# One second-level sum of an attention job by accumulating DMAs, a lead of three jobs, DMA transposes before the feed-forward, and six W2 buffers

## The chip, the cores and the metric

The kernel runs on one core of a Trainium2 chip, in one launch. The core has a matrix engine (TensorE, PE in the profile), a vector engine (VectorE, DVE), an activation engine (ScalarE, ACT), GpSimd (POOL) and a queue engine (SyncE, SP) that here only issues DMAs. Each of them runs its own list of instructions in order; semaphores make one wait for another. 16 DMA engines move data. The metric is the device time of one execution in microseconds (us).

## The reference

One transformer layer on 2048 tokens of width 1024, all in bf16, with 32 heads of width 32 and a feed-forward width of 3584:

```python
qkv = (layernorm(x) @ wqkv).reshape(B, S, 3, H, Dh)            # H = 32, Dh = 32
p = softmax(q @ k.T * Dh ** -0.5)                              # per head, 2048 x 2048
h = x + (p @ v) @ wo
h2 = h + gelu_tanh(layernorm(h) @ w1 + b1) @ w2 + b2           # F = 3584
```

The layer norms have no weights. Rounding of the variance and of its root follows bf16.

## The kernel before

**A planner writes the instruction lists.** The kernel first describes its whole work as tasks with an engine, a cost, a latency, the buffers that they read and write, and a priority (`Graph.add`). `Graph.schedule` then plays these tasks through in time and writes down the order on each engine; `assign` turns dependences into semaphore waits. What runs on the chip is that fixed order, with waits: if something is late on the chip, the engine that waits for it stands still, and all that follows in its list with it. Two tables of digits (`PV_BEGIN`, `PV_MUST`) and two of shifts (`GROUP_SHIFT`, `PRIO_SHIFT`) steer the order; they have no other effect.

**Attention.** A job is one block of 256 queries (`qb`, 0 to 7) with one group of four heads (`g`, 0 to 7): 64 jobs. A job has 8 rounds of 256 keys. In a round PE writes the scores of four heads with 8 matmuls (`qk`, line 941), ACT takes the exponential in two instructions of 128 x 1024 (line 952) into a buffer PT, and PE multiplies by V with 8 matmuls (`pv`, line 996). The scores use PSUM banks 0 to 5 as three units of two banks; a round takes two units, so PE can be about half a round ahead of ACT. Banks 6 and 7 serve everything else.

**Row sums.** The softmax denominators come from matmuls with a matrix of ones (`den`, line 1036). To need fewer of them, DVE first adds the two halves of a round's PT into a sum buffer PS (the first-level sum, line 1013), then adds PS buffers in pairs (the second-level sum, line 1019). A job has seven first-level sums, for rounds 0 to 6, and three second-level ones, for rounds 0+1, 2+3 and 4+5. Round 7 goes into `den` directly, with 8 matmuls instead of 4 per sum. There are three PS buffers. `Job.pv` writes this; `DIRECT` says how many of the last rounds go directly.

**Lead.** At the start the tokens come in 16 tiles of 128. DVE computes the layer norm of a tile (lines 715 to 741), PE transposes it (line 763), ACT or DVE copies it to `xnT` (lines 770 and 772; `LEAD_ACT` lists the ten tiles that ACT copies), and PE projects Q, K and V of head group 0. With each pair of tiles two more half-chunks of keys are there, and the rounds of jobs (0,0) and (1,0) are put in as their keys come. 50 warm-up matmuls (line 1262) stand in front. After the lead `ORDER` names the jobs that run between the remaining projections.

**Feed-forward.** It is spread as background work over the attention of later query blocks, one block of 256 tokens (a unit) at a time: `wo` (output projection and residual), `ln2` (second layer norm, PE transposes, and a DVE copy to `hnT`, line 772), `ffn1` (14 weight blocks of 512 KB, DVE adds the bias, and gelu with DVE and one ACT tanh), `ffn2` (two halves of 7 weight blocks of 512 KB, in a ring of seven buffers `a_w2r`). The last unit's feed-forward stands alone at the end, and so does part of the one before; its gelu runs on ACT. GpSimd only computes a power for the layer norms (line 736).

Of the kernel before, what the change touches and what calls it, by code (L numbers as in the profile page):

```python
# [13 lines left out]
BF = dt.bfloat16  # L14
F32 = dt.float32
# [21 lines left out]
class Task:  # L37
    __slots__ = ("eng", "fns", "occ", "lat", "deps", "prio", "kind", "mode", "left", "succ", "ready", "done",
                 "order", "inc", "flow", "value", "grp", "lane", "waits", "bytes", "acq", "rel", "whole")

    def __init__(self, eng, fns, occ, lat, prio, kind, mode):
        self.eng, self.fns, self.occ, self.lat = eng, fns, occ, lat
        self.prio, self.kind, self.mode = prio, kind, mode
        self.deps = set()
        self.succ = []
        self.left = 0
        self.ready = 0.0
        self.done = None
        self.order = None
        self.inc = False  # L50
        self.flow = None
        self.value = 0
        self.lane = None
        self.waits = ()
        self.bytes = 0
        self.grp = None
        self.acq = None
        self.rel = None
        self.whole = None


class Graph:
# [7 lines left out]
    def __init__(self, n_lanes):  # L70
        self.tasks = []
        self.regions = {}
        self.n_lanes = n_lanes
# [36 lines left out]
    def schedule(self, pick_pe, pool, switch=(0.11, 0.106, 0.1), dma_rate=340.0, dma_first=1.6, dma_tail=1.0, dma_issue=0.42,  # L110
# [9 lines left out]
        lanes = [None] * self.n_lanes  # L120
        state = {"mode": None, "dma": 0.0, "pace": 0.0}
# [21 lines left out]
        while n < total:  # L143
# [5 lines left out]
            for e in self.ENGS:  # L149
                while free[e] <= now + 1e-9:  # L150
# [12 lines left out]
                    else:  # L163
                        t = min(rd, key=lambda x: (x.prio, num[x]))
                        if up and t.prio > 0:

                            for (rt, _, u) in up[:6]:
                                if u.prio < t.prio and rt < now + 0.6 * t.occ:
# [17 lines left out]
                    if e == E.SP:  # L186
# [14 lines left out]
                        state["dma"] = s0 + t.bytes / dma_rate / 1e3  # L201
                        t.done = state["dma"] + dma_tail
# [34 lines left out]
    def assign(self, flows, lane_flows):  # L237

        for t in self.tasks:
            best = {}  # L240
            keep = set()
            for d in t.deps:
                if d.eng == E.SP:
# [8 lines left out]
        lane_n = [0] * len(lane_flows)  # L252
        for e in self.ENGS:
            c = 0
            for t in self.seqs[e]:
                if e == E.SP:
# [3 lines left out]
                    t.value = 16 * lane_n[t.lane]  # L260
                else:
# [43 lines left out]
        for i, s in enumerate(lane_flows):  # L305
            self.sems[("L", i)] = s

# [22 lines left out]
    def emit(self, e, obj):  # L330
        for t in self.seqs[e]:
# [5 lines left out]
            if t.inc:  # L337
                ins.then_inc(self.sems[t.flow], 16 if e == E.SP else 1)


PV_BEGIN = "6887668783765478677666734877585674766834855865775635885656674536"
PV_MUST = "2563656375427345237632753323452322425663763553734473555222232667"
GROUP_SHIFT = (
        "0:-229 1:131 2:136 6:-161 8:-202 9:133 11:142 14:17 15:-143 16:-115 17:-197 18:-131 20:-226 22:18 "
        "26:-18 28:-97 32:-17 33:177 34:-29 39:56 40:-11 42:55 44:53 45:81 46:22 48:243 50:-360 51:-22 "
        "55:-161 56:-142 57:-12 61:-20 66:-4 68:-18 69:18 72:-25 73:-7 76:-9 78:-61 83:-51 84:5 88:-36 "
        "89:-80 91:-37 92:-13 93:-18 94:6 95:125 98:-125 100:-193 101:-23 104:132 105:226 106:91 111:401 "
        "112:505 113:205 117:-165 118:182 120:-316 121:-313 122:-8 123:-383 124:-11 127:54 131:-14 133:-43 "
        "134:-32 135:-435 136:-33 138:-391 141:-7 145:-13 150:102 160:-184 163:3 165:232 166:-25 167:-29 "
        "169:-162 174:-10 175:592 176:-1 177:626 178:17 179:99 180:-167 182:-21 183:116 184:-46 185:11 "  # L350
        "186:24 187:-51 197:-74 198:-215 199:13 200:81 201:-20 202:4 207:-50 208:-4 209:172 211:-27 214:118 "
        "215:-55 216:-45 219:385 230:-13 231:14 232:-7 233:72 234:-5 235:78 236:-65 238:135 239:-593 240:29 "
        "241:-111 244:-185 245:112 247:-121 248:22 250:39 251:104 252:15 261:50 264:-4 268:220 270:-530 "
        "271:5 272:-920 273:1 274:-176 276:-54 277:91 279:24 281:31 293:171 294:13 295:123 296:-33 298:-6 "
        "299:111 300:113 301:2 305:321 308:34 310:17 311:10 313:52 315:-85 326:3 328:-4 329:-160 330:-11 "
        "331:-184 333:-150 334:102 335:-44 338:9 339:-99 341:74 342:48 344:-2 345:-172 347:170 349:-26 "
        "350:-28 352:-23 354:63 355:-74 356:-11 ")
PRIO_SHIFT = (
        "0:1 2:1 4:-1 6:-3 67:-1 68:-4 69:1 70:1 72:1 78:1 79:-3 80:1 81:-3 83:1 84:1 104:-2 125:-1 128:-3 "
        "129:-2 130:-1 132:-1 133:-1 154:1 167:-1 176:1 183:-1 187:-1 188:-1 228:-1 230:-1 234:-2 239:-4 "  # L360
        "250:-2 260:-3 264:-2 266:-2 276:-3 282:-1 307:-2 310:1 322:-3 330:-2 332:1 334:1 335:-1 344:1 353:1 "
        "356:-1 360:-1 369:2 370:1 371:2 373:-2 375:-1 378:-1 381:-1 406:2 415:3 417:1 418:2 420:-1 423:-1 "
        "426:3 427:1 446:4 462:1 511:-1 545:2 579:3 613:1 623:1 624:-1 627:1 637:-3 646:-1 649:1 651:1 "
        "652:-1 655:1 657:5 661:1 665:1 667:-1 670:1 672:1 676:1 684:2 686:1 698:-1 702:2 708:-1 710:-1 "
        "720:-1 722:-1 725:1 737:1 739:-1 753:-2 754:3 765:1 766:-2 772:-4 774:-1 778:2 788:1 789:-1 791:-1 "
        "792:-2 801:-1 810:3 870:1 936:-3 969:2 1003:-1 1020:-1 1037:-1 1040:1 1066:1 1086:-1 1089:-2 "
        "1097:-1 1102:-1 1103:-1 1114:-1 1126:1 1127:2 1130:2 1137:1 1138:3 1139:-1 1140:-1 1150:1 1168:-2 "
        "1186:1 1254:-1 1262:-1 1264:-1 1274:-3 1279:-1 1282:-1 1288:-1 1294:-1 1302:1 1303:1 1305:-1 "
        "1314:-1 1322:-2 1326:-2 1340:-1 1344:1 1346:-1 1358:-2 1394:1 1484:1 1485:-1 1494:2 1497:2 1508:-1 "
        "1515:-1 1519:1 1520:-1 1521:-1 1526:1 1528:-1 1531:1 1537:1 1540:2 1549:-2 1555:-3 1561:-3 1571:-1 "  # L370
        "1572:-1 1575:-3 1584:-1 1593:-1 1620:-1 1637:-2 1654:-1 1701:3 1710:-1 1716:-1 1732:1 1737:-1 "
        "1739:-3 1740:1 1742:-1 1748:1 1753:2 1756:-1 1760:-2 1762:-2 1765:2 1766:-1 1774:-1 1777:-2 1778:-1 "
        "1780:-1 1788:-1 1790:2 1791:3 1801:-1 1810:1 1828:-1 1837:-1 1854:1 1871:1 1888:2 1905:1 1908:1 "
        "1918:-1 1919:2 1928:1 1931:-2 1940:1 1943:1 1946:2 1949:3 1954:2 1955:-1 1956:-2 1968:1 1970:1 "
        "1982:1 1992:2 1998:1 2006:-1 2007:1 2008:1 2105:-1 2130:-1 2136:2 2142:1 2159:3 2166:1 2170:1 "
        "2171:1 2172:-1 2173:-1 2174:1 2187:-1 2196:-1 2200:1 2206:1 2211:-1 2212:1 2222:-1 2224:-1 2226:-2 "
        "2262:1 2271:-1 2274:2 2276:-2 2279:-1 2284:1 2288:1 2296:1 2297:-1 2300:3 2315:1 2319:-1 2320:-4 "
        "2323:-1 2326:1 2328:-2 2340:1 2343:-2 2348:1 2349:-3 2355:1 2361:-1 2367:-1 2373:1 2375:-3 2386:1 "
        "2398:1 2408:1 2410:-1 2420:-1 2440:-2 2465:-3 2493:1 2494:-1 2498:-7 2503:1 2512:-1 2513:-1 2516:-2 "
        "2517:-1 2518:1 2521:-1 2522:3 2544:1 2574:-1 2576:-2 2586:1 2595:1 2618:1 2636:-1 2655:-1 2656:3 "  # L380
# [1153 lines left out]
```

## Time and profile before

Three runs took 1078.71, 1082.22 and 5466.11 us; the median is 1082.22 us.

| | |
|---|---|
| profiled execution | 1079.89 us, its span 1078.0 us |
| instructions recorded | 38343 |
| busy: TensorE, ScalarE, VectorE, GpSimd | 1037.0, 1016.2, 887.6, 18.8 us |
| first exponential starts, last one ends | 17.69 us, 1017.66 us |
| VectorE, second-level sums (line 1019) | 191, 130.8 us |
| TensorE clock granted | 1.00 throughout |
| DMA moved | 173.93 MB, mean 161 GB/s |

Busy time is a union of intervals: an ACT instruction's record overlaps the next one's, so 1016.2 us of busy time do not say that no instruction came late. The page also shows the chain that ended last (followed back from the end), groups of instructions by line with the idle time before them and what ended it, and the median time of each kind of DMA from issue to landing.

### The profile page before, as it was taken

How to read it: one execution, taken by the hardware profiler on the slowest of the kernel's cores; microseconds unless marked ns; L12 is line 12 of the kernel's file. 1: busy time of each engine (PE TensorE's matmuls, PEld its weight loads, DVE VectorE, ACT ScalarE, POOL GpSimd, SP SyncE). 2: the span in 40 equal slices, each digit the busy share in tenths (PEclk: the TensorE clock that was granted, in tenths of full speed). 3: DMA queues.
4: the chain of work that ended last, by engine and by line, in shares of the span. 5: the costliest groups of instructions: out<-in, count | busy, mean ns of one | idle time of the engine just before them, and what ended most of it. 6: DMA issues, size and time to landing. Idle time of an engine off the chain costs nothing.

```text
span 1078.0 us, 38343 instructions
## 1 busy us (share of the span) xinstructions
PE 1037.0 (96%) x17162; PEld 586.8 (54%) x17162; DVE 887.6 (82%) x1737; ACT 1016.2 (94%) x1121; POOL 18.8 (2%) x35
## 2 busy tenths in 40 slices
PE   7889999999999999999999999999999999999998
PEld 5546555554446645654466457456645644564483
DVE  8888677777789997998789979988997997997711
ACT  4999999999999999999999999999999999999850
POOL 2000000000000000000000000000000000000000
DMA  7910010005656575754686667558575755987640
GB/s 196 256 60 3 13 49 2 2 2 175 205 153 204 149 224 167 220 164 132 222 259 183 189 197 203 163 173 260 150 222 184 210 150 162 290 258 236 192 153 20
DMA packets 265492, 173.93 MB, mean 161 GB/s; under 512 B 26864, under 2 KB 259952, under 8 KB 264944
## 3 DMA queue, kind: packets, MB, share of 16 engines
q1 hardware_dynamic: 265328, 171.48, 53.1%
q8 instruction: 135, 2.21, 0.8%
q14 instruction: 29, 0.24, 0.1%
HBM read 161.09 MB, written 10.35 MB: 159 GB/s over the span
## 4 chain that ended last, share of the span: by engine, by line
ACT 85%; PE 10%; DVE 3%; DMA 2%; issue 0%; SPq 0%; DVEq 0%
ACT PT L952 79%; PE ps L672 5%; ACT tg L1215 4%; PE ps L669 3%; ACT PX L952 1%; PE ps L941 1%; DMA a_w1r<-in_B_w_dram 1%; DVE st L715 1%; ACT xnT L770 1%; DMA xrb<-in_A_x_dram 0%; PE ps L996 0%; DVE PS L1013 0%; DMA a_w1r<-in_A_wo_dram 0%; DVE xb L741 0%; DVE gT L1192 0%
## 5 line engine op out<-in xcount | busy, mean ns | idle before, releaser
L952 ACT ACTIVATE PT<-ps 128x1024 bf16<-128x1024 f32 x1008 | 937.4, 1148 | 5.4 <-PE ps L941 5.2
L1013 DVE TENSOR_TENSOR PS<-PT 128x1024 bf16<-128x1024 bf16 x439 | 297.4, 684 | 78.1 <-ACT PT L952 52.1
L941 PE MATMUL ps<-QT,KT 32*128 32x256 bf16 x4096 | 203.6, 273 | 13.6 <-ACT PT L952 9.9
L996 PE MATMUL ps<-PT,V 128*32 128x256 bf16 x4032 | 160.5, 273 | 2.9 <-DVE gT L1192 1.1
L941 PEld LDWEIGHTS ps<-QT,KT 32*128 32x128 bf16 x4096 | 60.8, 92 | 170.0 <-ACT PT L952 157.8
L669 PE MATMUL ps<-hnT,a_w1r 128*128 128x256 bf16 x1197 | 148.1, 273 | 1.8 <-DMA a_w1r<-in_B_w_dram 0.7
L1019 DVE TENSOR_TENSOR PS<-PS 128x1024 bf16<-128x1024 bf16 x191 | 130.8, 685 | 3.4
L669 PE MATMUL ps<-a_w2r,gT 128*128 128x512 bf16 x510 | 125.7, 380 | 3.7 <-DVE hnT L772 1.2
L669 PEld LDWEIGHTS ps<-hnT,a_w1r 128*128 128x128 bf16 x1197 | 109.2, 98 | 35.3 <-issue 20.3
L996 PEld LDWEIGHTS ps<-PT,V 128*32 128x32 bf16 x4032 | 100.9, 96 | 37.5 <-issue 6.3
L666 PE MATMUL ps<-a_w2r,gT 128*32 128x512 bf16 x1096 | 80.2, 382 | 0.4 <-DVE gT L1192 0.2
L669 PEld LDWEIGHTS ps<-a_w2r,gT 128*128 128x128 bf16 x510 | 43.8, 98 | 61.9 <-issue 15.0
L1036 PE MATMUL ps<-PS,ones 128*32 128x256 bf16 x1020 | 70.5, 274 | 0.8 <-DVE PS L1013 0.5
L1192 DVE TENSOR_TENSOR gT<-ps,b1f 128x512 bf16<-128x512 f32 x98 | 66.7, 684 | 4.8 <-PE ps L669 2.4
L666 PE MATMUL ps<-hnT,a_w1r 128*32 128x256 bf16 x1484 | 54.5, 274 | 1.7 <-DMA a_w1r<-in_B_w_dram 0.6
L1215 ACT ACTIVATE tg<-tg 128x1024 bf16<-128x1024 bf16 x49 | 55.6, 1148 | 0.0
L669 PE MATMUL ps<-xnT,Wall 128*128 128x512 bf16 (+1 forms) x241 | 51.9, 345 | 2.5 <-ACT xnT L770 1.6
L669 PE MATMUL ps<-Wall,xnT 128*128 128x256 bf16 x345 | 45.6, 274 | 1.4 <-DVE KT L819 0.8
L666 PEld LDWEIGHTS ps<-hnT,a_w1r 128*32 128x32 bf16 x1484 | 36.3, 96 | 13.4 <-issue 11.2
L666 PE MATMUL ps<-xnT,Wall 128*32 128x512 bf16 x540 | 39.1, 381 | 0.6 <-DVE KT L819 0.6
L1244 DVE SCALAR_TENSOR_TENSOR b_ost<-ps,hch 128x512 bf16<-128x512 f32 x4 | 2.8, 692 | 44.7 <-PE ps L672 44.7
L669 PEld LDWEIGHTS ps<-Wall,xnT 128*128 128x128 bf16 x345 | 31.2, 98 | 12.7 <-issue 5.1
(101 smaller groups left out, 998.0 us busy)
## 6 DMA issues: line engine op xcount, KB each, us to landing
a_w2r<-in_B_w_dram SPq DMA_DIRECT2D x105, 512.0 KB, 4.8
a_w1r<-in_B_w_dram SPq DMA_DIRECT2D x98, 512.0 KB, 4.8
a_w1r<-in_A_wo_dram SPq DMA_DIRECT2D x32, 512.0 KB, 4.5
b_w1r<-in_B_w_dram SPq DMA_DIRECT2D x14, 512.0 KB, 5.0
a_w1r<-in_A_wqkv_dram SPq DMA_DIRECT2D x11, 512.0 KB, 4.0
xrb<-in_A_x_dram SPq DMA_DIRECT2D x16, 256.0 KB, 4.1
Wall<-in_A_wqkv_dram SPq DMA_DIRECT2D x16, 256.0 KB, 4.6
hch<-in_A_x_dram SPq DMA_DIRECT2D x16, 256.0 KB, 4.4
```

Of the source, the lines that this page charges most:

```text
L666: fns.append(lambda p, j=j: p.matmul(psum[32 * j:32 * j + 32, bi(bank), c0:c1], lhsT[:, 32 * j:32 * j + 32], rhs, start=start, stop=stop, ...
L669: t.whole = lambda p: p.matmul(psum[:, bi(bank), c0:c1], lhsT, rhs, start=start, stop=stop, skip_group_check=True)
L672: t = pe(lambda p: p.matmul(psum[:, bi(bank), c0:c1], lhsT, rhs, start=start, stop=stop), occ, reads=reads, writes=[bb(bank)], mode="full" ...
L715: return dve(lambda v: v.bn_stats(st_l[:, i, 6 * c:6 * c + 6], src), 0.6, reads=[B_src], writes=[B_stl[i][c]], prio=prio)
L941: return p.matmul(psum[:, 2 * us[h // 2] + h % 2, n * i:n * i + n], KT[32 * h:32 * h + 32, g, k0:k0 + P], QT[32 * h:32 * h + 32, qs, 0:n], ...
L952: act(lambda a, u=u, k=k: a.activation(pt(s)[:, k, :, :], psum[:, 2 * u:2 * u + 2, :], ACT.Exp, bias=0.0, scale=SCALE), 1024, reads=[B_ps[ ...
L996: fns.append(lambda p, i=i, h=h: p.matmul(psum[32 * h:32 * h + 32, bi(bank), 0:nq], V[:, g, nk * r + i, 32 * h:32 * h + 32], pt(s)[:, h // ...
L1013: dve(lambda v: v.tensor_tensor(PS[:, n, :, :], pairs[:, :, 0:256], pairs[:, :, 256:512], ALU.add), c_dve(1024, 2), reads=[B_PT[2 * s], B_ ...
L1019: dve(lambda v: v.tensor_tensor(PS[:, n, :, :], PS[:, n, :, :], PS[:, m, :, :], ALU.add), c_dve(1024, 2), reads=[B_PS[n], B_PS[m]], writes ...
L1036: fns.append(lambda p, h=h, rhs=rhs, i=i: p.matmul(psum[32 * h:32 * h + 32, bi(bank), nq:2 * nq], ones32[:, :], rhs, start=False, stop=las ...
L1192: drop(dve(lambda v: v.tensor_tensor(gT[:, fc:fc + 2, cs], psum[:, bi(bank), 0:2 * n].rearrange("p (f c) -> p f c", f=2), b1f[:, fc:fc + 2 ...
L1215: act(lambda a: a.activation(t, t, ACT.Tanh, bias=0.0, scale=math.sqrt(2.0 / math.pi)), c, reads=B_t, writes=B_t, prio=-1)
```

## The change

1. **Accumulating DMAs.** After the early jobs (`soft_from`, which holds for the last 44 of 64 jobs) the second-level sum of rounds 0+1 is no longer a DVE instruction. GpSimd issues a DMA from one sum buffer to the other that adds (`add_by_dma`), with six semaphores of its own; the planner books it with 1 us on GpSimd and 524,288 bytes on the DMA engines.
2. **Two more sum buffers**, `PSX`, used by the same jobs: five in all.
3. **Six `a_w2r` buffers instead of seven**, to make room. `w2_blocks` still loads seven blocks for a half before its matmuls are recorded, so the seventh goes into the first's buffer, and the matmuls for the first four 128-row chunks of W2 wait for the seventh load and read its data: of each half in that ring rows 0 to 511 of W2 are left out and rows 3072 to 3583 are used in their place as well. The number of instructions, loads and bytes is that of seven blocks. The one half that has another ring (`b_w2r`, the last unit's first) is untouched.
4. **DMA transposes.** For seven of eight units `ln2` no longer transposes with PE and copies with DVE; SP issues a transposing DMA from the normalised tile to `hnT` (14 in all).
5. **A new lead.** Three jobs, (0,0), (1,0) and (2,0), instead of two; their 24 rounds go into `den` directly, with no DVE sums. ACT copies four tiles to `xnT` instead of ten, and two K, two Q and one V half-blocks instead of one K and one Q. The first tile is loaded in two parts and the second straight after it, ahead of the Q weights; the first Q half-block and all K half-blocks are projected in pieces of 128 columns; 34 warm-up matmuls. Fourteen exponential buffers (PX) beside the PT ring instead of eight.
6. **Order.** `ORDER` has jobs of query blocks 2 and 3 for head group 1 as well, and takes the last three groups of blocks 0 and 1 one block after the other; all four tables of the planner are new.

```diff
@@ attention sums
     def DIRECT(qb, g):
-        return 0 if qb < DA else 1
+        return 16 if g == 0 and qb < DLEAD else 1
...
-                n = cnt["ps"] % NS
+                n = cnt["ps"] % (NS + NSX if soft_from else NS)
...
-                    dve(lambda v: v.tensor_tensor(PS[:, n, :, :], PS[:, n, :, :], PS[:, m, :, :], ALU.add), c_dve(1024, 2),
-                        reads=[B_PS[n], B_PS[m]], writes=[B_PS[n]], prio=-2)
+                    if soft_from and r < 2:
+                        add_by_dma(ps(n), ps(m), P * 4096, [B_PS[n], B_PS[m]], [B_PS[n]], -2)
+                    else:
+                        dve(lambda v: v.tensor_tensor(ps(n), ps(n), ps(m), ALU.add), c_dve(1024, 2),
+                            reads=[B_PS[n], B_PS[m]], writes=[B_PS[n]], prio=-2)
@@ new helper
+    def add_by_dma(out_ap, in_ap, nbytes, reads, writes, prio):
+        t = gr.add(E.Pool, lambda g: g.dma_start(out_ap, in_ap, accum_op=ALU.add), 1.0, 0.0, reads, writes, prio, nbytes=nbytes)
+        t.soft = True
+        return t
@@ buffers
+    NSX = 2
+    PSX, B_PSX = sb(ffn, "PSX", [P, NSX, 4, 256], BF, NSX)
+    B_PS = B_PS + B_PSX
-    R1 = Rings(([w1a[:, i, :, :] for i in range(4)], B_w1a), [ffn] * 7, [ffn] * 2, [ffn] * 2, "a_")
+    R1 = Rings(([w1a[:, i, :, :] for i in range(4)], B_w1a), [ffn] * 6, [ffn] * 2, [ffn] * 2, "a_")
@@ ln2
-                transposes(R.xb[s][:, :], R.B_xb[s], slot(), hnT[:, :, t * P:(t + 1) * P], B_hnT[t], "dve", 0)
+                dma(hnT[:, :, t * P:(t + 1) * P], R.xb[s][:, :], 500000, reads=[R.B_xb[s]], writes=B_hnT[t], prio=-1, flip=True)
@@ lead
-    N_WARM = 50
-    LEAD_ACT = [0, 1, 2, 3, 4, 6, 8, 10, 12, 14]
+    N_WARM = 34
+    LEAD_ACT = [0, 1, 2, 3]
...
-    x_tile(0, -6)
+    x_tile(0, -6, 2)
+    x_tile(1, -6)
     load_w(WQ, -5, 0, P)
-    x_tile(1, -5)
-    load_w(WK, -5, 0, P)
     x_tile(2, -5)
...
-    ORDER = [(2, 0), (3, 0)] + [(k, g) for g in range(1, G) for k in range(2)]
+    ORDER = [(3, 0)] + [(k, g) for g in range(1, G - LATE) for k in (range(4) if g < NEX else range(2))]
+    ORDER += [(k, g) for k in range(2) for g in range(G - LATE, G)]
...
-        for k, r in {0: [(0, 0)], 1: [(0, 1), (1, 0), (1, 1)]}.get(hc, [(0, hc), (1, hc)]):
-            lead.append((k, r, att.qk((k, 0), r, NR + r if k else None)))
+        for k, r in {0: [(0, 0)], 1: [(0, 1), (1, 0), (1, 1)], 2: [(0, 2), (1, 2), (2, 0), (2, 1), (2, 2)]}.get(hc, [(0, hc), (1, hc), (2, hc)]):
+            if (k, r) != (2, 7):
+                lead[k, r] = att.qk((k, 0), r, None if k == 0 else NR + r if k == 1 else NR + 8 + r if r < 6 else NR - 1)
...
+    soft_from.append(1)
     late_q(1, [g for g in range(2, G) if g not in made])
```

In the diff NS = 3, DLEAD = 3, LATE = 3, NEX = 2 and V_ACT = 1; R1 has the rings of w1 blocks, W2 blocks, normalised tiles and output tiles of all units but the last.

## The prediction, made before the changed kernel ran

> **What bounds the kernel now.** I read the page's first part, then the chain that ended last, then ScalarE alone in order of time.
>
> ```profile
> PE 1037.0 (96%) x17162; PEld 586.8 (54%) x17162; DVE 887.6 (82%) x1737; ACT 1016.2 (94%) x1121; POOL 18.8 (2%) x35
> ...
> ACT 85%; PE 10%; DVE 3%; DMA 2%; issue 0%; SPq 0%; DVEq 0%
> ```
>
> Two engines look full, but the chain runs along ScalarE for 85% of the span. The pieces of that chain give its pace:
>
> ```profile
> 60.47 170.65 ACT PT L952 x186
> 884.58 53.17 ACT PT L952 x58
> ```
>
> That is 0.917 us from one exponential to the next in both stretches, so a round costs 1.835 us whatever the others do. ScalarE's timeline shows both ends (start, length, what; in brackets the idle time before it):
>
> ```profile
> 10.90 1.02 ACT L770 ACTIVATE xnT<-ps 128x1024 bf16<-128x1024 bf16 x1 [8.89 <-PE ps L763]
> ...
> 17.69 1.02 ACT L952 ACTIVATE PT<-ps 128x1024 bf16<-128x1024 f32 x1
> ...
> 24.02 1.02 ACT L952 ACTIVATE PT<-ps 128x1024 bf16<-128x1024 f32 x1 [1.00 <-PE ps L941]
> ...
> 1014.69 2.97 ACT L952 ACTIVATE PT<-ps 128x1024 bf16<-128x1024 f32 x3
> ```
>
> So the time is three pieces: 17.7 us until the first exponential, 1000.0 us of ScalarE, and 60.3 us after it, in which TensorE finishes the last units. In the 1000.0 us stand 1024 exponentials, 49 tanh and 7 copies: 1080 x 0.917 = 990.4 us. Only 9.6 us there are real waits. Nothing that merely unloads TensorE, VectorE or GpSimd can gain more than that.
>
> **The change, part by part.** Against the profiled execution's 1079.9 us (span 1078.0 plus 1.9 around it), 2.3 us under the median of the three runs.
>
> *ScalarE's list* loses six copies of 1024 columns and gains three of 256. The six stood in the full stretch, at 0.917; for the short ones the record is 0.38 us, about 0.3 of pitch. 6 x 0.917 - 3 x 0.3 = 4.6 us less.
>
> *The start.* The second tile's load stood behind a weight load:
>
> ```profile
> 3.47 1.29 DVE L715 BATCH_NORM_STATS2 st<-xrb 128x6 f32<-128x512 bf16 x2 [3.47 <-DMA xrb<-in_A_x_dram]
> ...
> 6.31 0.69 DVE L715 BATCH_NORM_STATS2 st<-xrb 128x6 f32<-128x512 bf16 x1 [1.31 <-DMA xrb<-in_A_x_dram]
> ```
>
> 2.84 us apart for two loads of 256 KB; with the weights behind it the tile comes about 1.4 us earlier. The projections of half the columns can be done before the second tile is there; 8 matmuls of 256 columns took 1.05 us. Together -2.4 before the first exponential. The gaps after it (the third exponential only at 24.02) shrink too, by 0.5 as I take it. Bounds: Q weights that come too late eat all of it (0); both gaps gone entirely give -6. I take -3.
>
> *VectorE* loses 21 first-level sums (the three direct jobs) and 53 second-level ones (9 of these jobs, 44 replaced): 74 x 0.685 = 50.7 us; 14 copies to `hnT` (9.4 us) go, 6 copies to `xnT` (4.1) come: 56 us of 887.6. VectorE isn't on the path; what this can buy is the share of the 9.6 us in which scores came late because a bank or a sum did. 3.3 us of them lie before 60 us and are counted above. Of the other 6 I take 2 (bounds 0 and, with jitter of the pace, 9).
>
> *TensorE* loses 112 transposes (8.8 us busy) and 16 warm-up matmuls, and gains 3 x (64 - 24) = 120 matmuls with ones straight from PT; 520 of that kind are 25.3 us busy, so 5.8 us. All beside ScalarE. After the last scores the order leaves 14 more W2 matmuls of 512 columns (0.213 us of streaming each) and less of `pv` and `wo`: +1.6 us of work in the tail. The tail has gaps (ScalarE waits 3.4 us for its statistics at 1021), so I take +1, bounds 0 and 1.6.
>
> *The accumulating DMAs* are the unknown: the trace has none. What waits for each is a `den`, and behind that the whole of TensorE's list, scores included. How long may it take? In the order of the changed kernel the `den` stands 4 rounds of scores after its exponentials in 2 of 44 cases, 5 in 24, 6 in 13 and 7 in 5. Matched instruction by instruction with the trace of before, `den` at a distance of 4, 5, 6, 7 rounds started 6.0, 7.6, 9.7 and 11.6 us (medians) after its exponentials, and the first-level sum was done 0.8 us (median; three quarters within 1.7) after them. With 1.7 that leaves 4.3, 5.9, 8.0 and 9.9 us for the DMA. Its nearest rows (KB each, median us from issue to landing):
>
> ```profile
> xrb<-in_A_x_dram SPq DMA_DIRECT2D x16, 256.0 KB, 4.1
> a_w2r<-in_B_w_dram SPq DMA_DIRECT2D x105, 512.0 KB, 4.8
> x_scratch<-xnT SPq DMA_DIRECT2D x3, 1024.0 KB, 7.3
> ```
>
> It moves 256 KB, but reads two operands; the lower end is 4.1, the upper 7.3 plus the 1.0 us of GpSimd's longest instruction, 8.3. I take the 512 KB row, two operands' worth, plus 0.7 us (GpSimd's mean instruction): 5.5. A late `den` costs what exceeds one exponential of lead, 0.9 us. At 5.5: 2 x (1.2 - 0.9), under 1 us, taken as 0. At 8.3: 24 x (2.4 - 0.9) + 2 x (4.0 - 0.9) = 42 us.
>
> [...] The row first: GpSimd's power took 0.55 us at its shortest and up to 0.99 beside a busy VectorE:
>
> ```profile
> L736 POOL TENSOR_TENSOR denb<-tb,cexp x25: 550/688/992, 7.8 to 1025.1; 128x1 bf16<-128x1 bf16 x18, 128x2 bf16<-128x2 bf16 x7
> ```
>
> So a busy VectorE has delayed a GpSimd instruction by 0.44 us, no more; with one such delay the landing is 5.9 us and the sum stays. [...]
>
> *The DMA transposes* (14, 256 KB): from the normalised tile to the first `ffn1` matmul that reads it lie at least 7 rounds, 12.8 us, in the order; a load of 256 KB takes 4.1 and 1024 KB 7.3. Hidden: 0. SP stands at each until VectorE has the tile, and the weight loads queue behind. The weight blocks are issued 4 rounds (7.3 us) or more ahead, all but four, against a landing in 4.8; so 2.5 us of delay are free, and each us beyond costs up to 14.
>
> *Six W2 buffers*: a half's first matmul waits for its seventh load. The order has moved with it (the same distances of 4 rounds and more); no wait of TensorE for `a_w2r` is on the list of before. 0, at most 1 us for each of 15 halves.
>
> Sum: 1079.9 - 4.6 - 3 - 2 + 1 = 1071.3.
>
> **The rivals.**
>
> *First, slower: the accumulating DMAs land late and TensorE stands before `den`.* For: the distances are short (5 rounds in 24 of 44) and SP's DMAs already keep the engines 60 to 70% busy. Against: a 512 KB load lands in 4.8 us in the same traffic. Solving 24(x - 6.8) + 2(x - 5.2) = 32 us, it reaches +2% at a landing of 7.9 us; at 8.3 the time is 1071 + 42 = 1113. A delay repeated is one way there: five of 0.44 us, one after the other while VectorE is busy, make 5.5 into 7.7, and the loss into 24 x 0.9 + 2 x 2.5 = 27 us, 1098. I give this way 0.08 of the rival's 0.24, since VectorE is busy 82% of the time.
>
> *Second: loads behind the transposes come late.* A transpose that holds the queue for 4.5 us instead of 2.5 gives 14 x 2 = 28 us, 1099; 5 us would be 1106. Against: the mean DMA share leaves room. For: nothing in the trace shows what a transpose costs.
>
> *Third: the lead is VectorE's, and the rest gains nothing.* From 10 to 35 us VectorE was busy without a gap. A pair of tiles now asks 4 statistics, 2 normalisations, 2 copies of 1024 and one of 256 plus small ones, some 5.5 us, as much as the six exponentials it feeds (5.5). If it takes 6.5, six pairs starve ScalarE by 6 us: 1078, as before.
>
> **How the numbers follow.** Forecast (DMAs hidden) 0.55; third rival 0.15; first 0.24; second 0.06. Predicted time: the likeliest case, 1071. Low end: every wait in the middle gone and all of the start, 1079.9 - 4.6 - 6 - 9 = 1060. High end: the first rival's price at 8.3 us, 1113; about a tenth lies above it. The forecast's own range is 1060 to 1077. A measurement of this kernel can tell about 2% from no change. 2% below the median of 1082.2 is 1060.6, at the floor of my bounds: 0.06. 2% above is 1103.8: most of the first rival (0.19) and half of the second (0.03): 0.22. Within: 0.72.
>
> **What would show it.** First exponential near 15.3 us; ScalarE's pace at 0.917 or a little less; last exponential near 1009. TensorE's waits for a DMA into PS or PSX near zero; tens of us there mean the first rival, and then the stretch of the last 44 jobs is longer by just that. TensorE waits for `a_w1r` or `hnT` above 5 us mean the second. Gaps before exponentials between 20 and 60 us mean the third. I am wrong altogether if ScalarE's middle gets longer with none of these waits.

## The result, and the profile after

The changed kernel took 1089.24 us (median of four runs, 1087.88 to 1097.66) beside 1082.37 us of the kernel before: ratio 1.0082, 95% interval [1.006, 1.0105]. Ten more runs on another occasion gave 1.0049 [1.0029, 1.0068]. Weighted by their intervals the two make 1.006, some 6.5 us slower, against a forecast of 0.992 (1071.3 us from the profiled execution's 1079.9). The profiled execution took 1087.88 us, its span 1086.1.

The first page, with the busy times, the granted clock in 40 slices of 27 us, the chain that ended last, and a kind of accumulating DMA (KB each, median us from issue to landing):

```profile
PE 1025.8 (94%) x17729; PEld 588.4 (54%) x17789; DVE 842.6 (78%) x1657; ACT 1013.4 (93%) x1118; POOL 61.4 (6%) x80
...
PEclk9999999999999989999899999999999999999999
...
PE 44%; ACT 43%; DVE 6%; DMA 5%; issue 1%; SPq 0%; DVEq 0%
...
PS<-PS POOLq DMA_DIRECT2D x18, 256.0 KB, 5.2
```

VectorE is 45 us less busy, and nothing is faster for it. The chain has moved from ScalarE (85% before) to TensorE and ScalarE by halves. Two slices show a clock that before was at full speed everywhere. ScalarE's timeline gives the ends (start, length, what, in brackets the idle time before):

```profile
14.07 1.94 ACT L999 ACTIVATE PT<-ps 128x1024 bf16<-128x1024 f32 x2
...
1021.76 1.94 ACT L999 ACTIVATE PT<-ps 128x1024 bf16<-128x1024 f32 x2 [0.57 <-PE ps L988]
```

The exponentials begin 3.6 us earlier (17.69 before) and end 6.0 us later (1023.70 against 1017.66); the tail is 2.0 us longer. Matching the same exponential in both traces shows where the lead is lost:

| time before, us | 17.7 | 86 | 211 | 322 | 341 | 440 | 538 | 598 | 755 | 835 | 1016 |
|---|---|---|---|---|---|---|---|---|---|---|---|
| after minus before, us | -3.6 | -6.9 | -7.0 | -8.3 | -5.8 | -4.2 | -0.9 | +0.9 | +3.2 | +4.3 | +6.2 |

For 320 us the change is worth what was forecast. Then 14.3 us are lost in the 700 us in which the 44 accumulating DMAs, the DMA transposes and the six-buffer ring are at work. The way there is not even: between these columns the difference is -1.8 at 700 us and +2.3 at 960 us. (Profiles of one kernel differ: that of the second occasion lost 10.) The chain in order of time (start, length, what) names some of the places:

```profile
352.40 6.27 DMA PSX<-PSX
...
395.77 7.38 DMA a_w2r<-in_B_w_dram
...
723.12 7.64 DMA PS<-PSX
```

Five accumulating DMAs (two of them here) and one load of W2 stand on the path; before, no DMA into PS could. At the load, around 400 us, the table of stretches shows something more (start:end, length, then busy us and instructions of TensorE, its weight loads, VectorE, ScalarE and GpSimd, then granted clock, DMA share, GB/s):

```profile
394.74:398.15 3.41, 1.55 (x36) 0.58 (x34) 1.69 (x5) 3.41 (x6) 0.00 (x0) 1.00 1.09 381
398.15:401.57 3.42, 1.84 (x32) 0.80 (x36) 1.56 (x4) 3.42 (x5) 0.89 (x1) 0.50 1.05 361
401.57:404.98 3.41, 2.71 (x28) 0.96 (x21) 1.80 (x4) 3.32 (x4) 0.00 (x0) 0.50 0.47 92
...
524.45:527.86 3.41, 1.25 (x32) 0.41 (x24) 2.22 (x6) 3.41 (x5) 0.00 (x0) 1.00 0.92 265
527.86:531.28 3.42, 2.41 (x40) 1.03 (x42) 1.38 (x2) 3.42 (x5) 0.86 (x1) 0.50 0.91 259
```

Twice TensorE is busy for less than half of 3.41 us, and then runs at half clock for 6.8 us. In the kernel before it has work all the time around these places:

```profile
389.00:406.00 17.00, 16.93 (x254) 7.32 (x255) 16.03 (x37) 17.00 (x19) 1.40 (x2) 1.00 0.75 237
520.00:537.00 17.00, 16.99 (x296) 8.29 (x298) 12.50 (x23) 17.00 (x20) 0.00 (x0) 1.00 0.54 171
```

Its timeline in the changed kernel says what it lacked:

```profile
398.51 0.61 PE L988 MATMUL ps<-QT,KT 32*128 32x256 bf16 x8 [1.44 <-ACT PT L999]
400.34 0.61 PE L988 MATMUL ps<-QT,KT 32*128 32x256 bf16 x8 [1.22 <-ACT PT L999]
...
403.60 0.63 PE L691 MATMUL ps<-a_w2r,gT 128*128 128x512 bf16 x1 [0.70 <-DMA a_w2r<-in_B_w_dram]
```

From 396.67 to 400.88 us only scores are left to do, at ScalarE's pace; 24 `pv` and 8 more scores follow, and at 403.60 the first matmul of the next `ffn2` half finds its W2. The last matmul of the half before had ended at 390.5 us, the sixth and seventh load of the new half were issued from 394.84 us on, and the seventh landed at 403.2. In a ring of six the sixth load goes into the buffer of the earlier half's last block, so it can't be issued before that half has ended. TensorE's waits between 60 and 1020 us (in total, times, longest) complete the list of suspects:

```profile
PE ps L688 <- issue: 3.3, 3, 1.5
PE ps L1086 <- DMA PS<-PSX: 2.4, 2, 1.2
PE ps L1086 <- issue: 2.2, 2, 1.5
...
PE ps L1086 <- DMA PS<-PS: 0.8, 2, 0.6
PE ps L1086 <- DMA PSX<-PSX: 0.7, 1, 0.7
```

"issue" is a gap that no semaphore ended. The kernel before has no such line in this list; here they come to 10.9 us, but in the second profile of the same kernel to 2.4.

### The profile page after: what moved, and what is told of

Its sections match the earlier page's. It is cut to its first block, busy times and chain, and to the rows that moved or that the text cites. A ratio compares the mean times of both kernels' runs of the same rounds, so it can differ in the third digit from the quotient of the medians.

```text
span 1086.1 us, 39493 instructions
## 1 busy us (share of the span) xinstructions
PE 1025.8 (94%) x17729; PEld 588.4 (54%) x17789; DVE 842.6 (78%) x1657; ACT 1013.4 (93%) x1118; POOL 61.4 (6%) x80
## 4 chain that ended last, share of the span: by engine, by line
PE 44%; ACT 43%; DVE 6%; DMA 5%; issue 1%; SPq 0%; DVEq 0%
ACT PT L999 39%; PE ps L691 17%; PE ps L688 9%; PE ps L988 7%; PE ps L694 5%; PE ps L1043 5%; ACT tg L1265 2%; DMA PS<-PSX 2%; PE ps L1086 2%; ACT PX L999 2%; DMA xrb<-in_A_x_dram 1%; DVE PS L1060 1%; DMA PS<-PS 1%; DMA a_w2r<-in_B_w_dram 1%; DVE PSX L1060 1%
## 5 line engine op out<-in xcount | busy, mean ns | idle before, releaser
L1060 DVE TENSOR_TENSOR PS<-PT 128x1024 bf16<-128x1024 bf16 x302 | 206.8, 687 | 75.8 <-ACT PT L999 60.1
L691 PE MATMUL ps<-hnT,a_w1r 128*128 128x256 bf16 x1036 | 127.1, 273 | 2.0 <-DVE PSX L1060 0.9
L691 PEld LDWEIGHTS ps<-hnT,a_w1r 128*128 128x128 bf16 x1036 | 94.7, 98 | 29.6 <-issue 16.4
L1060 DVE TENSOR_TENSOR PSX<-PT 128x1024 bf16<-128x1024 bf16 x123 | 84.3, 686 | 31.8 <-ACT PT L999 25.8
L688 PE MATMUL ps<-hnT,a_w1r 128*32 128x256 bf16 x2128 | 76.0, 274 | 6.1 <-issue 3.3
L688 PEld LDWEIGHTS ps<-hnT,a_w1r 128*32 128x32 bf16 x2128 | 52.3, 96 | 20.1 <-issue 17.2
L1069 DVE TENSOR_TENSOR PS<-PS 128x1024 bf16<-128x1024 bf16 x86 | 59.1, 687 | 1.7
L1086 PE MATMUL ps<-PS,ones 128*32 128x256 bf16 x688 | 48.7, 274 | 5.2 <-DMA PS<-PSX 2.4
L691 PE MATMUL ps<-a_w1r,OT 128*128 128x512 bf16 x168 | 44.0, 380 | 1.4 <-DVE rr L1125 0.6
L765 POOL TENSOR_TENSOR denb<-tb,cexp 128x1 bf16<-128x1 bf16 (+1 forms) x26 | 21.2, 817 | 361.2 <-DVE tb L758 361.2
```

The lines of the kernel that those rows point to most:

```text
L688: fns.append(lambda p, j=j: p.matmul(psum[32 * j:32 * j + 32, bi(bank), c0:c1], lhsT[:, 32 * j:32 * j + 32], rhs, start=start, stop=stop, ...
L691: t.whole = lambda p: p.matmul(psum[:, bi(bank), c0:c1], lhsT, rhs, start=start, stop=stop, skip_group_check=True)
L765: pool(lambda g: g.tensor_tensor(denb[:, sl, 0], tb[:, sl, 0], cexp[:, 0:n], ALU.pow), 0.75 + 0.157 * n, reads=B_tb[sl] + [B_cexp], writes ...
L1060: dve(lambda v: v.tensor_tensor(ps(n), pairs[:, :, 0:256], pairs[:, :, 256:512], ALU.add), c_dve(1024, 2), reads=[B_PT[2 * s], B_PT[2 * s ...
L1069: dve(lambda v: v.tensor_tensor(ps(n), ps(n), ps(m), ALU.add), c_dve(1024, 2), reads=[B_PS[n], B_PS[m]], writes=[B_PS[n]], prio=-2)
L1086: fns.append(lambda p, h=h, rhs=rhs, i=i: p.matmul(psum[32 * h:32 * h + 32, bi(bank), nq:2 * nq], ones32[:, :], rhs, start=False, stop=las ...
```

## The experiments

Except for the three kernels with an order of their own, every kernel is planned as the changed kernel is, keeps its order on every engine but for the edit, and derives its waits from the buffers that the edited work uses. Ratios are to the kernel before on the same chip; 0.001 is 1.08 us.

### One suspect at a time

**The additions the other way round**, so that `den` reads a buffer that no DMA writes:

```diff
-        t = gr.add(E.Pool, lambda g: g.dma_start(out_ap, in_ap, accum_op=ALU.add), 1.0, 0.0, reads, writes, prio, nbytes=nbytes)
+        t = gr.add(E.Pool, lambda g: g.dma_start(in_ap, out_ap, accum_op=ALU.add), 1.0, 0.0, reads, writes, prio, nbytes=nbytes,
+                   real=(reads[:1], reads[1:]))
```

> The changed kernel with every instruction at its place; the 44 accumulating DMAs add the other way round (the later buffer into the earlier one), so the ones-matmul that follows reads a buffer that no DMA writes and no longer waits for it. The traffic is the same. This leaves the earlier half of two rounds out of 44 denominators. Theory 1 (the time is lost where the ones-matmul waits for the accumulating DMA: about 5 us of ScalarE's time in the changed profile, at 358.7, 730.8, 828.8, 938 and 969.7 us): 1083 to 1084 us, ratio to the kernel before 1.001 to 1.004, and TensorE's waits for DMA into PS and PSX are gone. Rival (the time is lost to the traffic that the DMAs add, or elsewhere in the new order): 1088 us, ratio 1.006 to 1.010, though those waits are gone.

Measured 1.0036 [1.002, 1.0052], 1085.49 us; `den` waits for no DMA. Against the first measurement of the changed kernel (1.0082) that is 5 us, against the weighted 1.006 it is 3 us, just clear of the noise. The waits cost something, not the whole.

**The sums back on VectorE**, in the changed order:

```diff
+    for t in gr.tasks:
+        if t.soft:        # the 44 DMAs: from GpSimd's list into VectorE's, as tensor_tensor
+            gr.seqs[E.Pool].remove(t)
+            t.eng, t.soft, t.fns, t.occ, t.lat = E.DVE, False, [t.whole], 0.6, 0.135
```

> The changed kernel with the 44 accumulating DMAs replaced by the VectorE additions of the kernel before, each put in VectorE's row where the plan has the DMA start; all else in the same place. Nothing is left out. Theory 1 (only the waits cost): 1083 to 1084 us. Theory 2 (the added traffic also holds back TensorE's instructions: the gaps at 370, 430, 557, 668 and 752 us, some 6 to 7 us, end just after a packet of an instruction queue): those gaps go too, 1076 to 1079 us, ratio 0.994 to 0.998. Rival (VectorE, with 44 x 0.6 us = 26 us more to do, comes late in this order): no better than 1088 us.

Measured 1.0074 [1.0051, 1.0096], 1089.07 us: the rival's time. In an order made for the DMAs the kernel is no faster without them: either VectorE's 26 us cost as much as the DMAs did, or neither costs much; this run does not tell. "Issue" gaps of 0.5 to 1.1 us near 560, 670 and 965 us are there without any accumulating DMA, so they do not need its traffic.

**The seventh W2 load sent to DRAM**, and **plain copies for the DMA transposes**:

```diff
-            dma(R.w2[s][:, :, :], B_w2[512 * q:512 * q + 512, c] ...
+            dma(w2d[:, :, :] if R is R1 and q == FC // 4 - 1 else R.w2[s][:, :, :], B_w2[512 * q:512 * q + 512, c] ...
```

```diff
-                return s.dma_start_transpose(out_ap, in_ap)
+                return s.dma_start(out_ap, in_ap.rearrange("p (c t) -> p c t", t=P))
```

> The changed kernel with every instruction at its place, but the seventh load of each half of the second FFN matmul goes to a buffer in DRAM, so the first matmul of a half no longer waits for it. The same number of bytes is read. The seventh block of W2 is left out and the first used twice (the changed kernel leaves out the first). Theory 3 (the six-buffer ring makes halves begin late, TensorE idles at 395 to 401 and 524 to 529 us, and the clock is halved for 6.8 us after each): no halving at 398 and 528 us, 1085 us, ratio 1.002 to 1.006. Rival (the halved clock comes from something else, or costs nothing): 1088 us, ratio 1.006 to 1.010.

> The changed kernel with the 14 DMA transposes replaced by plain DMA copies of the same bytes between the same buffers at the same places. The transposition is left out. Theory 4 (the transposes hold SyncE for 1.2 to 3.6 us each and disturb the other transfers): 1086 us or less, ratio below 1.006. Rival (they cost nothing, as forecast): 1088 us, ratio 1.006 to 1.010.

Measured 1.0048 [1.0028, 1.0067] and 1.0065 [1.0043, 1.0087]: neither can be told from the changed kernel. The transposes are cleared. The first says less than it was meant to: the clock was halved at 403 and 529 us as before, because the order, which was kept, still puts the half's matmuls behind the thin stretch.

### The clock

In all four of these profiles the clock is halved near 400 and near 530 us. Across the twelve runs with plain copies the time goes from 1083.5 us at a mean clock of 0.994 to 1094.8 at 0.986 (another at 0.994 took 1089.1). So the next edit keeps TensorE busy in the two stretches and changes nothing else:

```diff
+        for x in at:      # the groups of scores in the stretch, once the bank b is free
+            fs = [lambda p, b=b: p.matmul(psum[:, b, :], ident[:, :], KT[:, 0, 0:512], start=True, stop=True, skip_group_check=True)
+                  for _ in range(4)]
+            q.insert(q.index(x) + 1, d)
```

> The changed kernel with every instruction at its place, and 36 more matmuls of 128x512 that compute nothing that is used: four behind each of nine groups of scores in the two stretches (about 391 to 401 and 521 to 530 us) in which TensorE has only scores because the next half of the second FFN matmul waits for the seventh load of a six-buffer ring. They write a PSUM bank that is free then. In all five profiles of the changed order the granted clock is 0.5 for 3.4 to 10.2 us behind each of these stretches, and across the runs so far a mean clock lower by 0.001 goes with about 1 us more. Theory 5 (the stretches cost by the halved clock): no halving near 400 and 530 us, mean clock 0.996 to 0.998 where the changed kernel has 0.990 to 0.992, 1081 to 1084 us, ratio 1.000 to 1.004. Rival (the halved clock falls into slack; the stretches themselves cost): 1087 to 1089 us, ratio 1.006 to 1.010, although the clock stays.

Measured 1.0018 [1.0, 1.0037], 1083.29 us, mean clock 0.997 over the runs (0.991 for the changed kernel's ten). The same stretches of this kernel:

```profile
396.80:400.20 3.40, 3.40 (x56) 1.43 (x55) 0.88 (x3) 3.40 (x5) 0.00 (x0) 1.00 1.10 374
...
526.40:529.80 3.40, 3.05 (x41) 1.19 (x40) 2.25 (x7) 3.40 (x5) 0.00 (x0) 1.00 0.94 312
```

36 matmuls for nothing make the kernel 4 to 5 us faster (1.006 to 1.0018; the interval of the difference reaches from 2 to 7 us). That keeping TensorE busy there saves time is shown by the edit. The traces say where. Matched exponential by exponential with the kernel before, six profiles of this order without the filling and six with it lose on the average

| time before, us | 322 to 392 | 392 to 440 | 440 to 520 | 520 to 598 | 598 to 1016 |
|---|---|---|---|---|---|
| without the filling, us | 2.1 | 0.9 | 1.5 | 3.5 | 5.1 |
| with it, us | 2.8 | 0.7 | 1.6 | 0.9 | 5.0 |

So some 2.6 us of the gain stand in the second stretch, and the first gains next to nothing: half clock near 400 us cost little here. The 5 us behind 598 us are lost with the filling too. (Without: the changed kernel twice and the four above; with: this one and the five below that contain the filling.)

> The two edits together: 36 matmuls in the two stretches, and accumulating DMAs that add the other way round, so that no ones-matmul waits for one (the earlier half of two rounds is left out of 44 denominators). Theory 1 and theory 5, if they are two separate losses: 5 us and 5 us off the changed kernel's 1088 us, 1076 to 1079 us, ratio 0.995 to 0.998. Rival (both measure one loss): 1083 us, no less than either alone, ratio 1.001 to 1.004.

Both edits: 0.9997 [0.9982, 1.0012], 1081.10 us. The second takes 2.3 us more off, less than the 5 expected of it and by itself within the noise of the two intervals, but in line with the 3 us that it took off alone against the weighted ratio. The filling in turn takes 4.2 us off the kernel without the waits (1.0036 to 0.9997), which is clear of the noise and repeats its gain. Two losses, not one, is what fits both pairs.

> The first of these kernels (36 matmuls in the two stretches) and 44 matmuls of 128x128 more, unused as well, in three gaps of the lead (about 21, 34 and 36 us), where the changed order's profiles have the clock at 0.5 for 3.4 us from 23 us on and again from 38 us on. Theory 5: another 3.4 to 6.8 us at full clock in the lead, about 2 to 4 us less than with the two stretches alone, mean clock above 0.998. Rival (the lead's halving falls into waits for data, or the added matmuls hold the lead up by what they save): the same time as with the two stretches alone, within 1 us.

Filling gaps of the lead as well gave 1.0053 [1.0033, 1.0072], 1087.62 us, though the profile has no halving in the lead. That is not the gain of the theory, and not the rival's "same within 1 us" either: it is 4 us slower than without this filling. At the exponential of 86 us its profile is not ahead (-5.5 against -6.2 us), so the halving in the lead cost nothing that shows. It loses the time later: 14.8 us from 322 us on (in an execution of 1090.68 us), against 7.6 without, where the two kernels have the same instructions in the same order. Why is open. It is a caution for all readings here: an edit in the lead moved the time by as much as the filling gained.

**The half's own matmuls in the stretch**, with the seventh load sent to DRAM as above:

```diff
+        moved = group[:5 * len(at)]     # group: the half's matmuls; at: the groups of scores in the stretch
+        for k, x in enumerate(at):
+            i = q.index(x) + 1
+            q[i:i] = moved[5 * k:5 * k + 5]
```

> The kernel whose seventh W2 load goes to DRAM (1.0048 of the kernel before with the changed kernel's order; the seventh block of W2 is left out and the first used twice), with one more edit: the first 15 and the first 10 matmuls of the two halves that stood behind the two thin stretches are moved up into them, five behind each group of scores; their blocks of W2 are the first to third, which are there. Theory 3 (the stretches are empty because a half may not begin before its seventh load): no halving of the clock near 400 and 530 us, mean clock 0.996 to 0.998, 1080 to 1083 us, ratio 0.998 to 1.002. Rival (something else holds the half up, so the matmuls wait at their new place): a halving near 400 or 530 us as before, 1086 us or more, ratio 1.004 or above.

> The changed kernel itself, for a closer interval: 1087 to 1090 us, ratio 1.006 to 1.010, a halved clock near 400 and 530 us.

Measured 1.0034 [1.0018, 1.005] and, for the changed kernel again, 1.0049. This settles nothing: the moved matmuls did not wait for W2, but near 395 us a `den` waited 1.5 us for its DMA, and the window before 397 us was thin again. That the ring empties the stretches rests on the trace (the wait for `a_w2r` at 403.6 us), not on an edit.

### What else the accumulating DMAs cost

**No second sums at all** for the 44, with the two stretches filled:

```diff
+    gr.tasks = [t for t in gr.tasks if not t.soft]
+    for t in gr.tasks:
+        t.deps = {d for d in t.deps if not d.soft}
```

> The changed kernel with the 36 unused matmuls in the two stretches and without the 44 accumulating DMAs: nothing adds those two buffers, no ones-matmul waits for a DMA, and 11.5 MB less is moved (the earlier half of two rounds is left out of 44 denominators). All else is at its place, as in the kernel with the DMAs adding the other way round, which took 0.9997 of the kernel before. Theory 6 (the traffic of the accumulating DMAs makes the weight loads late, and TensorE's waits for a_w1r and a_w2r of 0.7 to 1.4 us near 406, 431, 665, 760 and 816 us come from it): 3 to 4 us less, 1077 to 1079 us, ratio 0.995 to 0.998, those waits gone. Rival (the new order asks for these loads late by itself): 1081 us, ratio 0.998 to 1.001, the waits still there.

Measured 0.997 [0.9956, 0.9985], 1079.41 us: 3 us less than with the DMAs whose result nobody waited for (0.9997 [0.9982, 1.0012]), just clear of the noise. But TensorE still waits 2.6 us for `a_w2r` and `a_w1r`. In the one profile of the kernel with those DMAs it waits 6.5 us for them, in that of the filling alone 2.7, so the time is theory 6's, and single profiles neither show its mechanism nor exclude it. VectorE, too, waited for those DMAs before it could reuse a sum buffer (8.2 us in the changed profile). Which of the two makes the 3 us stays open.

**Readers put later**, with the two stretches filled:

```diff
+        want = t.ready + 8.5            # t: the accumulating DMA, d: the den that reads its sum
+        k = next(k for k in range(i + 1, len(q)) if q[k] is last or begin(q[k]) >= want and ...)
+        q.insert(k - 1, q.pop(i))
```

> The changed kernel with the 36 unused matmuls in the two stretches, its accumulating DMAs as they are, and 30 of the 44 ones-matmuls that read their sums put later in TensorE's list (by 0.1 to 5.6 us), so that the order has 8.5 us or more between the last first-level sum and its reader. Nothing is left out. Theory 1 (the DMAs cost by those waits alone, and these depend on the distance): as with the additions the other way round, 1080 to 1082 us, ratio 0.998 to 1.001, against 1.0018 with the 36 matmuls alone; waits for DMA into PS and PSX gone. Rival (a sum buffer that is held longer makes VectorE late, or the wait moves): 1083 us or more, ratio 1.001 to 1.004.

Measured 1.0127 [1.0107, 1.0147], 1095.32 us: the rival, and 12 us worse than with the readers in their place. VectorE's waits between 300 and 1020 us:

```profile
DVE PSX L1077 <- PE ps L1103: 13.3, 12, 2.8
DVE PS L1077 <- PE ps L1103: 12.8, 15, 2.4
```

Line 1103 is `den`, line 1077 the first-level sum that needs its buffer. In the changed kernel these waits are 4.4 us. Five buffers are too few to give the DMA more time, and `den` at its place is too early for the slow ones.

### An order of its own

Two kernels keep the lead, the transposes and the job order (with the two more columns of `OT`, the buffer of attention results, that it takes), and go back to seven W2 and three sum buffers; one has VectorE's sums, the other the DMAs. Their shift tables are new.

> The lead, the DMA transposes and the two OT columns of the change, but seven W2 buffers and three sum buffers as in the kernel before, all second-level sums on VectorE, and an order of its own (new shift tables). Nothing is left out. If the loss is that of the six-buffer ring (by the halved clock) and of the accumulating DMAs, the forecast's lead is what is left: the profile starts 3 us and runs on 7 to 8 us ahead of the kernel before, no halving of the clock between 60 and 1010 us, 1071 to 1076 us, ratio 0.990 to 0.995. Rival (DMA transposes, or any order made anew, cost what the changed kernel lost): 1082 us or more, ratio 1.000 or above.

> The changed kernel with its 44 accumulating DMAs, but seven W2 buffers in place of six and three sum buffers in place of five (the two do not fit together), in an order of its own. Nothing is left out. If the six-buffer ring cost 7 us and the waits for the accumulating DMAs 2 to 5 us: 1076 to 1080 us, 2 to 5 us above the same with VectorE's sums, and no halving of the clock between 60 and 1010 us. Rival (the DMAs cost nothing once the order is made for them, VectorE's 26 us are the gain the change was credited with): the same as with VectorE's sums or less. Rival (three sum buffers are too few for sums that take 5 us): 1085 us or more, with VectorE's first-level sums waiting for a buffer.

Measured 1.0 [0.9983, 1.0016] (1081.48 us) and 1.0096 [1.007, 1.0122] (1092.55 us). The second is the rival with three buffers, as one line shows (VectorE's waits again):

```profile
DVE PS L1056 <- DMA PS<-PS: 28.5, 19, 4.1
```

The first refutes me: without ring and DMAs the forecast's time does not come. Its profile, of an execution of 1086.81 us, is 8.7 us ahead at 211 us, and then loses it. Two stretches of it:

```profile
399.16:402.57 3.41, 1.06 (x14) 0.33 (x11) 3.34 (x9) 2.69 (x3) 0.00 (x0) 1.00 1.21 213
402.57:405.98 3.41, 3.25 (x30) 0.93 (x34) 0.94 (x3) 1.61 (x2) 0.00 (x0) 0.50 0.65 193
```

Here a load of W2 came 2.4 us late with seven buffers, and the clock was halved all the same. All its waits for weights are 8.5 us. So a third order was made on loads that take 1.4 us longer:

> As the kernel with seven W2 buffers and all sums on VectorE (ratio 1.000; TensorE waited 8.5 us for a_w2r and a_w1r, up to 2.4 us at once), but with an order made on loads that take 1.4 us longer. Nothing is left out. Theory 7 (the order asked for weights too late): waits for a_w2r and a_w1r below 2 us, no halved clock between 60 and 1010 us, 1072 to 1077 us, ratio 0.991 to 0.996. Rival (what is lost is not the loads but gaps that no semaphore ends and the new order's VectorE waits): 1080 us, ratio 0.998 or above, though the loads are in time.

The loads are in time (1.1 us of waits) and the clock is 1.00 until the tail, but the ratio is 0.9993 [0.9981, 1.0005], 1081.56 us: the rival. Its profile starts 3.1 us earlier, ends its exponentials 2.7 us earlier and has a tail 2.7 us longer. ScalarE stands idle 4.6 us more between them than before (11.4 us against 6.8). Matched with the kernel before, it is still 8.3 us ahead at 1000 us, a little more than was forecast for start and list; 5.6 us of that go in the next 10 us, and 2.7 in the tail. Its timelines (TensorE, then ScalarE) show the largest piece:

```profile
996.97 3.97 PE L681 MATMUL ps<-a_w2r,gT 128*32 128x512 bf16 x68
...
1001.21 3.77 ACT L992 ACTIVATE PT<-ps 128x1024 bf16<-128x1024 f32 x4 [2.81 <-PE ps L1036]
```

From 980 to 1020 us TensorE is busy for 9.8 of every 10 us or more (in the kernel before for 9.1 to 10.0). 68 matmuls of W2 stand before the next scores, and ScalarE waits 2.81 us. At the end of this kernel TensorE has no slack, so exponentials that come earlier only meet it earlier.

**Fewer instructions**, on the kernel of 0.9997: more runs of narrow matmuls done wide.

```diff
-            if k == 0 or sum(x.occ for x in run[k:]) >= 3.0:
+            if k == 0 or sum(x.occ for x in run[k:]) >= 0.8:
```

> The kernel with the 36 matmuls and the additions the other way round (0.9997 of the kernel before; the earlier half of two rounds is left out of 44 denominators), but with more of its runs of four 32-column matmuls done as one of 128 columns: 840 TensorE instructions less, same products, same places. Theory 2 (TensorE's gaps that no semaphore ends are instructions that come late, because narrow matmuls use them up faster than they come): those gaps of 0.5 us and more (2 us in that kernel, 6.6 in the changed one, none in the kernel before) go, 1078 to 1080 us, ratio 0.996 to 0.999. Rival (they are chance, or fall into slack; the wide matmuls do not overlap with their neighbours in other columns): no gain, ratio 0.999 or above.

Measured 1.0038 [1.0015, 1.0062], 1085.25 us: 4 us worse, and its profile has 7.7 us of "issue" gaps (1.4 in the profile of the kernel that it changes). Theory 2 fails as a remedy; what these gaps cost isn't separated.

## Why the prediction was wrong

It missed the point, 1071 us, by 16 to 18 us, and the direction: faster was forecast, and the kernel is slower. The time lay in the wide range, 1060 to 1113 us, on the side of the first rival, and outside the forecast's own, 1060 to 1077.

- **The start and ScalarE's list: right.** The forecast had -7.6 us for both; the trace has -8.3 at 322 us. The start gave more than was taken for it (first exponential at 14.1 us, not 15.3) and the list less. It lost six copies and gained three, as counted (1077 ScalarE instructions from the first exponential to the last in place of 1080), but the three short ones held it for 2.1 us with the gaps behind them, not 0.9: some 3.4 us rather than 4.6.
- **"0, at most 1 us for each of 15 halves": the step that failed first.** Six W2 buffers were read as a load's distance, and the wait for it is indeed 0.7 us at 403 us. What the sum left out is TensorE with little else to do meanwhile, and the clock after that: 4 to 5 us by the filling, of which the traces place 2.6 in the stretch at 528 us. That the ring empties these stretches is argued from the order of loads and matmuls in the trace; the two edits that went for it did not show it.
- **The accumulating DMAs at 0: the second.** The landing was forecast at 5.5 us and took 5.1 at the median, but 3.2 at the least and 7.6 at the most. The sum took one landing time where landings spread; 5 of 44 readers waited, all for landings above 6.2 us, 5 us of ScalarE's time in that profile and 2 to 3 us by the edits. The first rival was the right mechanism at a small part of its 42 us. Another 3 us come from the DMAs or what waits behind them; no step had that. (The rival's "60 to 70% busy" DMA engines were 0.53 busy in the mean from 60 to 1000 us of the profile before.)
- **GpSimd's delay of 0.44 us: not shown to be VectorE's.** The prediction put the difference between the shortest and the longest of GpSimd's powers, 0.55 and 0.99 us, down to a busy VectorE. In the trace of before a power of 0.55 us stands wholly beside a VectorE instruction too (402.90 us; the statistics run from 402.80 to 403.48). In the changed profile GpSimd took 0.86 us to issue an accumulating DMA, 1.05 at the most.
- **VectorE's relief, -2: did not come.** VectorE is 45 us less busy, not 56, and that bought nothing measurable; where its sums were put back, in an order made for that, the time was the same (1.0).
- **DMA transposes at 0: right.** Plain copies were no faster. SP took 1.2 to 3.6 us to issue one, and no wait of TensorE for `hnT` is on the list of the changed profile.
- **The tail, +1: it was +2.0.** (The W2 matmuls behind the +1 follow one another every 0.216 us in the trace of before, not 0.213: 25 of them take 5.56 us from 1050.75 us on, one alone 0.38.) In the third kernel with an order of its own, which has neither the ring of six nor the accumulating DMAs, it is +2.7. "All beside ScalarE" is the step that fails there: ScalarE's lead of 8.3 us is kept up to 1000 us, and TensorE, busy for 9.8 of every 10 us from 980 us on, does not finish earlier.

By the edits the account is 5 us for the clock, 2 to 3 for `den`, 3 for the DMAs otherwise: from 1.006 down to 0.997. Each of the three is known to about 2 us either way, and two other edits moved the time by 4 us without a reason found. The other 5 us to the forecast's 0.992 are the tail's extra 1, the list's missing 1, the relief of 2 that did not come, and waits for weights and gaps of the new orders, which no run here separates. The sentence "I am wrong altogether if ScalarE's middle gets longer with none of these waits" was nearly the case: from the first exponential to the last it got 9.7 us longer (14.3 from 322 us on), with 3.9 us of waits for a DMA into PS and PSX.

## What to carry to other kernels

A buffer taken out of a ring can cost more than the wait that it adds (0.70 us at 403.60 us here): look at what the engine has to do in that wait, since two stretches of 3.41 us with only 1.55 and 1.25 us of work for TensorE were each followed by 6.83 us at half clock. The accumulating DMAs landed in 3.2 to 7.6 us: set the slowest landing, not the median, against the smallest distance, and count the buffers that a larger distance would hold. A forecast that takes time off one engine should say whose waits it shortens; an engine off the path gave nothing here for 45 us. And a lead in one engine's list was worth here only what the engine that finishes last could follow: 8.3 us at 1000 us, and a ratio of 0.9993 at the end.

## What the hardware did that I had not expected

**The clock was halved in pieces of 3.41 us.** In the changed profile it was at half for 3.41 us from 22.69 us on and for 6.83 us from 398.15 and from 527.86 us on; from start to start that is 110 and 38 such pieces. In the piece before each, TensorE's matmuls were busy (by the profile) for 0.47, 0.45 and 0.37 of the time; the next lowest at full clock, 0.55 from 749.73 us on, was followed by full clock. In 14 profiles with a halving before the tail, all halvings began and lasted on a grid of that length, which lay differently in each execution. Of their pieces at full clock from 10 us on, all 20 in which TensorE's matmuls were busy for less than 0.42 of the time were followed by half clock, none of over 4000 above 0.63 was, and 18 between 0.44 and 0.63 were while others were not. The longest gap near 398 us was 1.44 us.

**Gaps without a releaser ended after an instruction packet.** TensorE's five gaps of this kind above 0.7 us in the changed profile, where a mere sequence of matmuls breaks off, as here (its timeline),

```profile
428.40 0.40 PE L688 MATMUL ps<-hnT,a_w1r 128*32 128x256 bf16 x7
430.30 0.82 PE L688 MATMUL ps<-hnT,a_w1r 128*32 128x256 bf16 x21 [1.51 <-issue]
```

each ended 2.2 to 2.4 us after a packet of 16 KB on the instruction queue began. That the instructions came late is argued from this; the edit with 840 fewer did not remove them, and the second profile of the same kernel has three above 0.5 us, none above 1.0.

**An accumulating DMA of 256 KB between two buffers in SBUF** took GpSimd 0.86 us to issue and 3.2, 5.1 and 7.6 us (least, median, most) to land; a DMA transpose of 128 x 1024 bf16 between two buffers 2.7, 4.7 and 7.9 us.
